# Longformer attention and its feed-forward stage on one core: transposes between another pair's score products, clears on ScalarE, one scatter per batch, casts spread by pair

## The chip, the core and the metric

The kernel runs on one core of a Trainium2 chip. The core has TensorE (PE, with its weight loads as PEld), VectorE (DVE), ScalarE (ACT), GpSimd (POOL) and SyncE (SP), each with a queue of its own that it takes in order; SP and POOL issue the DMAs. The metric is the time of one execution on the device in microseconds, lower is better; a kernel's time is the median of several runs.

## The reference

```python
# q, k, v: [8 batches, 8 heads, 576 positions, 64], global_idx: 8 positions
scores = matmul(q, k.T) / 8
mask = (abs(i - j) <= 32) | is_global[i] | is_global[j]
attn = softmax(where(mask, scores, -1e9))
x = matmul(attn, v)                  # to [4608 tokens, 512]
r = maximum(x @ w_in, 0)             # w_in [512, 2048]
out = (s * r * r + b) @ w_out        # w_out [2048, 512]
```

## The kernel before

**Tiling.** A *pair* is two heads of one batch; pairs are numbered 0 to 31, four to a batch. A pair's keys lie in five chunks of 120, with the 8 global rows put in front of each. For each chunk one score product (`qk`, L449) multiplies the chunk's keys `kt` with a window of the pair's queries `qbd`; ScalarE takes the exponential (`e`), VectorE multiplies with the mask (`em`). Then `pv` (L476) makes 28 products: `em` with V and with ones, into one PSUM tile `po`. `norm_steps` follow: logarithm of the sums on ScalarE (`ln`), its negative exponential (`rep`), and on VectorE the normalised output into `xt`, plus `gs`, the sums for the global queries.

**Preparation of a pair.** `trans_a` and `trans_b` transpose K and Q of a pair on PE into a PSUM tile `pst`; VectorE, and for batches 0 and 1 ScalarE for half of q, evacuate it to `kt` and `qbd`. For batches 0 and 1 `select_globals` and `select_v` pick the global rows by products (`psg`, `psv`), and a small DMA on SP puts the selected rows of V (`gv`) into `vx`. Three `qbd` buffers hold zeros in the half that belongs to the other head, and rows 0 to 7 of `natv` are zero at first; memsets on VectorE write these.

**Loads.** K and Q of batches 0 and 1 come through POOL's DMA queue, already cast (`load_six`). From batch 2 on, SP loads K, Q and V in float32 to `natk`, `natq`, `natv` (`fetch`: 40 loads of half a batch's heads each, and three fills with the global rows that 24 gathers on POOL have put aside). ScalarE casts K and Q (L262), POOL casts V (L258).

**Second stage.** `moe_quanta` yields 288 quanta. For each of nine tiles of 512 tokens, 16 quanta compute `psh` (L546, four products or more, then ReLU on ScalarE and a square on VectorE) and 16 compute a quarter of `pso` (L561), with an output store on SP after each fourth. From pair 8 on, every pair runs eight of them, one behind each of its steps. The global queries' outputs are put into `xt` by the scatter in `finish_batch`: 8 small copies on POOL (L524), and a quantum that reads `xt` waits for them.

**Order.** All five engines take the order in which the code emits. `run_pair` has eight steps: five score products, `trans_a` of the next pair, `trans_b` and the selections, `pv`. What VectorE does for a step is put into `later` and emitted one step behind. The sums of w_out's rows for the bias need all of w_out in float32: eight pieces `wst`, two per pair in pairs 6 to 9, issued by SP into two buffers and added by VectorE a pair later (L698, L700).

Of the kernel before, what the change touches and what calls it, by code (L numbers as in the profile page):

```python
# [9 lines left out]
FP32 = mybir.dt.float32  # L10
# [53 lines left out]
def kernel(  # L64
# [96 lines left out]

    new_casts(0)
# [56 lines left out]
    nc.vector.memset(nat["v"][0:NG], 0.0)  # L219
# [266 lines left out]
    def norm_steps(p):  # L486
# [6 lines left out]

        def s1():
            nc.scalar.activation(ln[:], po[:, LQ : 2 * LQ], AF.Ln)  # L495
            later.append(
                lambda: nc.vector.tensor_reduce(
                    out=gs[:, hp],
                    in_=po.rearrange("p (h c j) -> p h j c", h=2, c=NCH)[:, :, HB : HB + NG, :],
                    axis=AX.X, op=OP.add,  # L500
                )
            )
# [278 lines left out]
```

## Time and profile before

| | |
|---|---|
| median of 3 runs | 420.28 us (420.23 to 421.6) |
| the profiled execution | 419.66 us, of which the trace's span is 418.0 us |
| PE busy | 355.6 us, 85% of the span |
| DVE busy | 243.7 us, 58% |
| ACT busy | 216.1 us, 52% |
| POOL busy | 67.2 us, 16% |
| mean granted clock of PE | 0.958 of full speed |

The three runs and the profiled execution lie within 0.5% of each other. The shares are averages over the whole span. The stretches, the waits and single instructions are in the rows further down: times count from the start of the span, "idle before" is what an engine waited just before an instruction, and behind the arrow stands what ended that wait.

### The profile page before, as it was taken

How to read it: one execution, taken by the hardware profiler on the slowest of the kernel's cores; microseconds unless marked ns; L12 is line 12 of the kernel's file. 1: busy time of each engine (PE TensorE's matmuls, PEld its weight loads, DVE VectorE, ACT ScalarE, POOL GpSimd, SP SyncE). 2: the span in 40 equal slices, each digit the busy share in tenths (PEclk: the TensorE clock that was granted, in tenths of full speed). 3: DMA queues.
4: the chain of work that ended last, by engine and by line, in shares of the span. 5: the costliest groups of instructions: out<-in, count | busy, mean ns of one | idle time of the engine just before them, and what ended most of it. 6: DMA issues, size and time to landing. Idle time of an engine off the chain costs nothing.

```text
span 418.0 us, 8890 instructions
## 1 busy us (share of the span) xinstructions
PE 355.6 (85%) x3323; PEld 215.0 (51%) x3354; DVE 243.7 (58%) x595; ACT 216.1 (52%) x401; POOL 67.2 (16%) x150
## 2 busy tenths in 40 slices
PE   2596483979925889989998999999999999999994
PEld 2364242544513545765685578557755764554442
DVE  5946272658607785875676577667666774332421
ACT  1346251666412853795488558836953872530610
POOL 5830595100211001110111020002101001000000
PEclk9998596999975999999999999999999999999999
DMA  8999625975895137953781587069601001101001
GB/s 153 177 206 211 110 39 119 151 199 159 155 164 160 45 126 152 147 143 88 151 181 48 126 161 181 1 146 154 169 27 51 27 2 52 50 2 76 26 32 69
DMA packets 113775, 46.33 MB, mean 111 GB/s; under 512 B 99044, under 2 KB 106212, under 8 KB 113732
## 3 DMA queue, kind: packets, MB, share of 16 engines
q1 hardware_dynamic: 105412, 38.91, 41.0%
q0 software_dynamic: 8320, 6.86, 10.5%
q8 instruction: 26, 0.43, 0.4%
q14 instruction: 17, 0.14, 0.1%
HBM read 42.77 MB, written 9.73 MB: 126 GB/s over the span
## 4 chain that ended last, share of the span: by engine, by line
PE 44%; issue 14%; SPq 13%; DMA 10%; DVE 8%; ACT 6%; POOL 3%; POOLq 0%; ACTq 0%; DVEq 0%
PE pso L561 23%; PE psh L546 14%; SPq L295 7%; SPq L306 6%; DMA natk<-in_k_dram 4%; PE po L476 3%; ACT r L553 3%; PE pss L449 3%; DMA win_t<-in_moe_w_in_dram 3%; DMA natv<-in_v_dram 2%; DVE g L556 2%; DVE qbd L397 2%; PE pst L360 2%; ACT e L453 1%; DVE wsum L700 1%
## 5 line engine op out<-in xcount | busy, mean ns | idle before, releaser
L546 PE MATMUL psh<-xt,win_t 128*128 128x512 bf16 (+7 forms) x1018 | 147.1, 290 | 12.3 <-POOL xt L524 11.6
L561 PE MATMUL pso<-wout_t,g 128*128 128x512 bf16 x551 | 137.7, 379 | 2.6 <-issue 1.9
L553 ACT ACTIVATE r<-psh 128x512 bf16<-128x512 f32 x144 | 87.4, 620 | 75.6 <-PE psh L546 73.7
L453 ACT ACTIVATE e<-pss 128x384 bf16<-128x384 f32 (+1 forms) x160 | 75.4, 483 | 83.7 <-PE pss L449 68.7
L546 PEld LDWEIGHTS <-win_t 128*128 128x128 bf16 x1024 | 85.8, 99 | 61.0 <-issue 21.8
L556 DVE TENSOR_TENSOR g<-r 128x512 bf16<-128x512 bf16 x144 | 64.9, 455 | 53.8 <-ACT r L553 51.8
L561 PEld LDWEIGHTS <-g 128*128 128x128 bf16 x576 | 54.1, 98 | 59.4 <-issue 3.5
L456 DVE TENSOR_TENSOR em<-e,mask 128x384 bf16<-128x384 bf16 (+1 forms) x160 | 55.3, 348 | 28.7 <-ACT e L453 27.0
L449 PE MATMUL pss<-qbd,kt 128*128 128x384 bf16 (+1 forms) x160 | 51.2, 331 | 16.3 <-ACT e L453 8.7
L575 DVE SCALAR_TENSOR_TENSOR osb<-pso,s_bc,bias_row 128x512 f32<-128x512 f32 x32 | 23.9, 748 | 42.0 <-PE pso L561 42.0
L524 POOL COPY xt<-xg 128x4 bf16 x72 | 15.2, 210 | 181.5 <-DVE xg L522 177.5
L258 POOL CAST vx<-natv 128x1280 bf16<-128x1280 f32 (+1 forms) x20 | 21.3, 1077 | 98.5 <-DMA natv<-in_v_dram 45.7
L397 DVE COPY qbd<-pst 64x640 bf16<-64x640 bf16 (+1 forms) x56 | 29.4, 525 | 0.3
L507 DVE TENSOR_TENSOR xt<-po,rep 128x600 bf16<-128x600 f32 x32 | 25.0, 781 | 6.8 <-ACT rep L505 6.8
L449 PEld LDWEIGHTS <-kt 128*128 128x128 bf16 x160 | 15.7, 100 | 25.1 <-DVE qbd L397 6.3
L495 ACT ACTIVATE ln<-po 128x640 f32<-128x640 f32 x32 | 22.5, 705 | 5.4 <-PE po L476 5.4
L505 ACT ACTIVATE rep<-ln 128x640 f32<-128x640 f32 x32 | 24.4, 764 | 0.1
L476 PEld LDWEIGHTS <-vx 128*64 128x64 bf16 x448 | 17.0, 118 | 14.3 <-issue 5.1
L476 PE MATMUL po<-em,vx 128*64 128x160 bf16 (+3 forms) x448 | 21.7, 237 | 2.5 <-DVE xt L507 1.6
L476 PE MATMUL po<-em,onesb 128*64 128x160 bf16 (+2 forms) x448 | 21.4, 237 | 0.0
L360 PE MATMUL pst<-ident,cq 128*128 128x128 bf16 x120 | 10.8, 222 | 11.7 <-ACT e L453 11.7
L700 DVE TENSOR_TENSOR wsum<-wsum,wst 128x512 f32<-128x512 f32 x14 | 9.6, 685 | 14.4 <-DMA wst<-in_moe_w_out_dram 14.4
(77 smaller groups left out, 209.9 us busy)
## 6 DMA issues: line engine op xcount, KB each, us to landing
out_dram<-osb SPq DMA_DIRECT2D x32, 256.0 KB
natq<-in_q_dram SPq DMA_DIRECT2D x108, 60.0 KB
natk<-in_k_dram SPq DMA_DIRECT2D x48, 120.0 KB
natv<-in_v_dram SPq DMA_DIRECT2D x48, 120.0 KB
wst<-in_moe_w_out_dram SPq DMA_DIRECT2D x8, 512.0 KB
natv<-in_v_dram SPq DMA_DIRECT2D x16, 150.0 KB
win_t<-in_moe_w_in_dram POOLq DMA_DIRECT2D x4, 512.0 KB, 10.0
wout_t<-in_moe_w_out_dram POOLq DMA_DIRECT2D x4, 512.0 KB, 12.8
```

The costliest lines, as they stand in the source:

```text
L295: eng.dma_start(out=nat[t][NG : NG + n, c, h0 : h0 + nh], in_=src[t][bi, h0 : h0 + nh, KC * c : KC * c + n].rearrange("h s d -> s h d"),)
L306: eng.dma_start(out=nat["q"][r : r + n, c, h0 : h0 + nh], in_=q[bi, h0 : h0 + nh, a : a + n].rearrange("h s d -> s h d"),)
L397: eng(out=o, in_=i)
L449: nc.tensor.matmul(ps[:], ktile[p][:, P * c : P * c + P], qbufs[p % 3][:, :, LO[c] : HI[c]])
L453: nc.scalar.activation(e[:], ps[:], AF.Exp, scale=SCALE)
L456: later.append(lambda: nc.vector.tensor_mul(em[:], e[:], masks[c]))
L476: nc.tensor.matmul(po[D * hh : D * hh + D, a : a + n], onesb[:] if part else vx[:, c, 2 * hp + hh], emt[(p, c)][:, hh, x : x + n], start=k ...
L507: lambda: nc.vector.tensor_tensor(out=xt[:, hp].rearrange("p (c a j) -> p c a j", c=NCH, a=2), in0=halves(po[:, 0:LQ]), in1=halves(rep[:]) ...
L546: nc.tensor.matmul(psh[:, d0 : d0 + n], win_t[:, a, f * P : f * P + P], xts[bi][:, a, x0 : x0 + n], start=(a == 0 and j == 0), stop=(a == ...
L553: nc.scalar.activation(r[:], psh[:], AF.Relu)
L556: later.append(lambda g=g, r=r: nc.vector.tensor_mul(g[:], r[:], r[:]))
L561: nc.tensor.matmul(pso[:], gl[f][:, u * P : u * P + P], wout_t[:, f], start=(f == 0), stop=(f == 15),)
```

## The change

`first_pair` replaces `run_pair` for batch 0: the next pair's transposes and selections stand between this pair's score products, and for pairs 0 to 4 the transposes' PSUM tile comes from the pool of the second stage. ScalarE clears `qbd` and `natv` by copies of a zero column. Pair 4 is prepared right behind batch 0, with no quantum ahead of it; batch 0 is scattered once, before pair 4 (before: there and again in pair 4). The memset of `natv`'s last rows goes. Loads of V for batch 1 are spread over pairs 1 to 3. `wst` is issued on POOL's queue. `fetch` takes half a batch at a time, and the casts of K and Q, two heads at a time, move to the last pair of the batch before and the first of the same batch. In batch 1 six quanta run per pair (before: four ahead of pair 4, then five per pair).

```diff
+    zero = const.tile([P, 1], FP32)
+    nc.vector.memset(zero[:], 0.0)
+
+    def clear(ap, n):
+        nc.scalar.copy(out=ap, in_=view(zero[0 : ap.shape[0]], [0, n]))
+
+    def clear_q(t):
+        clear(t[0:D, 1], LQ)
+        clear(t[D:P, 0], LQ)
+
+    clear_q(qbufs[0])
+    clear(nat["v"][0:NG].rearrange("p c h d -> p (c h d)"), NCH * H * D)
+    clear_q(qbufs[1])
+    clear_q(qbufs[2])
...
-    nc.vector.memset(nat["v"][0:NG], 0.0)
...
-    nc.vector.memset(qbufs[0][0:D, 1], 0.0)
-    nc.vector.memset(qbufs[0][D:P, 0], 0.0)
...
-    cast_v(G, 0, 0, 2)
     for hp in (2, 3):
         load_six("k", 0, hp)
         load_six("q", 0, hp)
+    cast_v(G, 0, 0, 2)
     cast_v(G, 0, 2, 2)
-    for j in range(4):
+    for j in range(2):
         nc.gpsimd.dma_start(
-            out=win_t[:, :, 512 * j : 512 * j + 512],
-            in_=w_in2[:, :, 512 * j : 512 * j + 512],
+            out=win_t[:, :, 1024 * j : 1024 * j + 1024],
+            in_=w_in2[:, :, 1024 * j : 1024 * j + 1024],
         )
...
     def trans(t, p):
         bi, hp = divmod(p, 4)
-        ps = ps_s.tile([P, LQ], BF16, tag="s", name="pst")
+        if p < 5:
+            ps = ps_m.tile([P, LQ], BF16, tag="moe", name="pst")
+        else:
+            ps = ps_s.tile([P, LQ], BF16, tag="s", name="pst")
...
-    def finish_batch(bi):
-        xt, gs = xts[bi], gsums[bi]
-        xg = nrm.tile([P, 4, NG], BF16, tag="xg", name="xg", bufs=2)
-        rec = nrm.tile([P, 4, NG], FP32, tag="rec", name="rec", bufs=1)
-        nc.vector.reciprocal(out=rec[:], in_=gs[:, :, 1])
-        nc.vector.tensor_tensor(out=xg[:], in0=gs[:, :, 0], in1=rec[:], op=OP.mult)
+    def scatter(bi):
+
         for i in range(NG):
             nc.gpsimd.tensor_copy(
-                out=xt[:, :, ds(greg_p[i], 1)], in_=xg[:, :, i : i + 1]
+                out=xts[bi][:, :, ds(greg_p[i], 1)], in_=xgs[bi][:, :, i : i + 1]
             )
...
             elif s == 5:
-                if hp == 0 and bi > 0:
-                    later.append(lambda: finish_batch(bi - 1))
+                if hp == 0 and bi > 1:
+                    later.append(lambda: scatter(bi - 1))
...
+    def first_pair(p):
+
+        if p == 0:
+            open_batch(0)
+        for s in range(NCH):
+            prev, later[:] = list(later), []
+            qk(p, s)
+            if s in (0, 2):
+                step()
+            if p < 3:
+                if s == 1:
+                    trans_a(p + 1)
+                elif s == 2:
+                    trans_b(p + 1)
+                    select_globals(p + 1)
+                elif s == 3:
+                    select_v(p + 1)
+            for f in prev:
+                f()
+        flush()
+        pv(p)
+        pending.extend(norm_steps(p))
...
-    def casts_for(bi):
-
-        return (
-            {1: [lambda: cast(A, "k", bi, 0, HG)], 4: [lambda: cast(A, "q", bi, 0, HG)],
-             5: [lambda: cast_v(G, bi, 0, HG)]},
-            {1: [lambda: cast(A, "k", bi, HG, HG)], 4: [lambda: cast(A, "q", bi, HG, HG)],
-             5: [lambda: cast_v(G, bi, HG, HG)]},
-        )
+    def casts_for(bi, h0):
+
+        c = lambda t, h: (lambda: cast(A, t, bi, h, 2))
+        return {
+            0: [c("k", h0)], 2: [c("q", h0)], 5: [c("k", h0 + 2)], 6: [c("q", h0 + 2)],
+            4: [lambda: cast_v(G, bi, h0, HG)],
+        }
...
-    for t in qbufs[1:]:
-        nc.vector.memset(t[0:D, 1], 0.0)
-        nc.vector.memset(t[D:P, 0], 0.0)
     for p in range(4):
-        run_pair(p, Z, p < 3)
-        if p == 2:
-            for h in range(H):
-                load_v_head(1, h)
+        first_pair(p)
+        for h in ((), (0, 1), (2, 3, 4), (5, 6, 7))[p]:
+            load_v_head(1, h)
+    cast_v(G, 1, 0, 2)
+    step()
+    trans_a(4)
     flush()
-    while pending:
-        step()
-        flush()
-    finish_batch(0)
+    step()
+    trans_b(4)
+    flush()
+    select_globals(4)
+    select_v(4)
+    scatter(0)
+    flush()
...
-    for t in "kqv":
+    for t in "kq":
         nc.vector.memset(nat[t][PADROW:P, NCH - 1], 0.0)
...
     quanta[0] = 32
-    for _ in range(3):
-        Q()
-        flush()
-    trans_a(4)
-    trans_b(4)
-    select_globals(4)
-    select_v(4)
-    Q()
-    flush()
...
-        nc.sync.dma_start(out=wt[:], in_=w_out2[:, 2 * j : 2 * j + 2])
+        nc.gpsimd.dma_start(out=wt[:], in_=w_out2[:, 2 * j : 2 * j + 2])
...
         if bi == 1:
-            nq = [0, 1, 1, 0, 1, 0, 1, 1]
+            nq = [0, 1, 1, 1, 0, 1, 1, 1] if hp else [0, 0, 1, 1, 1, 1, 1, 1]
...
+        if hp == 3 and bi + 1 < B:
+            new_casts(bi + 1)
+            ex = casts_for(bi + 1, 0)
+        if hp == 0 and bi > 1:
+            ex = casts_for(bi, HG)
         if p == 5:
-            new_casts(2)
-            fetch(2)
-        if hp >= 2 and bi + 1 < B:
-            ex = casts_for(bi + 1)[hp - 2]
+            fetch(2, 0)
+        elif p == 6:
+            fetch(2, HG)
+        elif bi > 1 and hp < 2 and bi + 1 < B:
+            fetch(bi + 1, HG * hp)
         if p in (7, 8, 9, 10):
             more, adds = adds, []
-            for s, f in zip((2, 3, 6, 7), more):
+            for s, f in zip((1, 3, 4, 7), more):
                 ex.setdefault(s, []).append(f)
```

What moves is shown at three places of the order, for each before and then with the change. The numbers behind names are buffers.

VectorE in pair 1, from its first mask product to what it does for pair 2 (`kt`, `qbd` and the selected rows from `psg`; `gv`), before:

```order
L456 TENSOR_TENSOR em_496<-e,mask_344 128x320
L456 TENSOR_TENSOR em_501<-e,mask_346 128x384
L497 TENSOR_REDUCE gs<-po 128x16
L456 TENSOR_TENSOR em_508<-e,mask_348 128x384
L456 TENSOR_TENSOR em_515<-e,mask_350 128x384
L507 TENSOR_TENSOR xt<-po,rep 128x600
L456 TENSOR_TENSOR em_522<-e,mask_352 128x320
L375 COPY kt<-pst 128x5x120
L397 COPY qbd_111<-pst 64x5x2x60
L415 CAST kt<-psg 128x5x8
L420 CAST qbd_111<-psg 64x5x8 x2
L439 CAST gv<-psv 8x128
```
With the change:

```order
L470 TENSOR_TENSOR em_496<-e,mask_348 128x320
L509 TENSOR_REDUCE gs<-po 128x16
L470 TENSOR_TENSOR em_502<-e,mask_350 128x384
L389 COPY kt<-pst 128x5x120
L470 TENSOR_TENSOR em_525<-e,mask_352 128x384
L528 TENSOR_TENSOR xt<-po,rep 128x600
L411 COPY qbd_111<-pst 64x5x2x60
L429 CAST kt<-psg 128x5x8
L434 CAST qbd_111<-psg 64x5x8 x2
L470 TENSOR_TENSOR em_573<-e,mask_354 128x384
L453 CAST gv<-psv 8x128
L470 TENSOR_TENSOR em_592<-e,mask_356 128x320
```
The evacuations for the next pair stood behind the pair's last mask product; now they stand between the mask products, and the last one comes behind `gv`.

SP from the first half's fills in batch 2's fetch on, before (`vx` from `gv` is the small DMA for pairs 6 and 7, `wst` a piece of w_out):

```order
L326 DMA natk<-gsk 8x5x512
L326 DMA natq<-gsq 8x5x512
L326 DMA natv<-gsv 8x5x512
L295 DMA natk<-in_k_dram 120x4x64 x4
L295 DMA natk<-in_k_dram 96x4x64
L306 DMA natq<-in_q_dram 60x4x64 x9
L306 DMA natq<-in_q_dram 36x4x64
L295 DMA natv<-in_v_dram 120x4x64 x4
L295 DMA natv<-in_v_dram 96x4x64
L440 DMA vx_108<-gv 8x5x128
L696 DMA wst<-in_moe_w_out_dram 128x2x512 x2
L440 DMA vx_108<-gv 8x5x128
```
With the change, from the small DMAs for pairs 4 and 5 on:

```order
L454 DMA vx_108<-gv 8x5x128 x2
L306 DMA natk<-in_k_dram 120x4x64 x4
L306 DMA natk<-in_k_dram 96x4x64
L317 DMA natq<-in_q_dram 60x4x64 x9
L317 DMA natq<-in_q_dram 36x4x64
L306 DMA natv<-in_v_dram 120x4x64 x4
L306 DMA natv<-in_v_dram 96x4x64
L337 DMA natk<-gsk 8x5x256
L337 DMA natq<-gsq 8x5x256
L337 DMA natv<-gsv 8x5x256
L454 DMA vx_108<-gv 8x5x128
```
The small DMA for pair 6 stood behind both halves of the fetch and now stands behind the first; the pieces `wst` are no longer in SP's queue.

POOL behind the 24 gathers of batch 1, before: the end of the second scatter of batch 0 (`xt_358`), the casts of V for batch 2 and the start of batch 1's scatter (`xt_997`):

```order
L524 ISA
L524 COPY xt_358<-xg_1119 128x4
L258 CAST vx0_107<-natv_106 128x5x256 x2
L524 ISA
L524 COPY xt_997<-xg_1833 128x4
```
With the change, from the last gather on; `xt_960` is batch 1's output:

```order
L329 DMA gsv_276<-in_v_dram 6x8x64
L726 DMA wst_1383<-in_moe_w_out_dram 128x2x512
L726 DMA wst_1385<-in_moe_w_out_dram 128x2x512
L726 DMA wst_1571<-in_moe_w_out_dram 128x2x512
L726 DMA wst_1573<-in_moe_w_out_dram 128x2x512
L269 CAST vx0_107<-natv_106 128x5x256
L726 DMA wst_1714<-in_moe_w_out_dram 128x2x512
L726 DMA wst_1716<-in_moe_w_out_dram 128x2x512
L269 CAST vx0_107<-natv_106 128x5x256
L539 ISA
L539 COPY xt_960<-xg_1754 128x4
```
The second scatter is gone, and the pieces `wst` stand in this queue, two of them ahead of the cast and the scatter of batch 1.

## Rows read from the trace of the kernel before

**Rows 1.** Windows (from:to, length, busy us and instructions): seven stretches

```profile
core 0: us, PE busy (x) PEld busy (x) DVE busy (x) ACT busy (x) POOL busy (x), PEclk, DMA share, GB/s
0.00:12.87 12.87, 3.10 (x58) 2.61 (x58) 7.95 (x27) 1.94 (x2) 8.08 (x21) 1.00 0.95 158
12.87:22.62 9.75, 6.65 (x90) 4.49 (x90) 7.60 (x20) 2.78 (x6) 7.43 (x11) 1.00 1.18 182
22.62:42.88 20.26, 15.63 (x215) 10.07 (x214) 12.11 (x33) 10.85 (x23) 2.23 (x3) 0.89 1.24 208
42.88:57.20 14.32, 7.37 (x73) 3.62 (x74) 6.23 (x18) 4.49 (x7) 10.75 (x23) 0.68 0.53 82
57.20:110.62 53.42, 42.32 (x460) 23.73 (x468) 32.70 (x85) 27.56 (x52) 15.45 (x34) 0.94 0.66 142
110.62:143.63 33.01, 19.84 (x180) 11.80 (x179) 14.60 (x36) 15.33 (x29) 3.06 (x5) 0.79 0.62 140
143.63:155.82 12.19, 10.45 (x81) 5.29 (x82) 10.65 (x24) 7.58 (x13) 0.00 (x0) 1.00 0.23 87
```

**Rows 2.** Windows: two pairs without casts, two with casts

```profile
311.48:330.14 18.66, 18.34 (x178) 11.50 (x179) 12.04 (x31) 9.68 (x20) 1.62 (x8) 1.00 0.15 57
174.48:194.81 20.33, 19.21 (x187) 11.85 (x188) 14.42 (x35) 16.19 (x28) 1.25 (x1) 1.00 0.37 96
```

**Rows 3.** Timeline (start, us, engine, line, operation) of the start

```profile
6.49 2.19 DVE L219 MEMSET natv<- 8x2560 f32 x1 [0.46 <-issue]
...
8.08 0.69 PE L348 MATMUL pst<-ident,cq 96*64 96x96 bf16 x12 [1.03 <-DMA cq<-in_q_dram]
...
11.37 0.76 DVE L397 COPY qbd<-pst 64x600 bf16<-64x600 bf16 x1
...
12.16 0.65 ACT L397 COPY qbd<-pst 64x600 bf16<-64x600 bf16 x1 [10.00 <-DVE qbd L397]
...
12.80 2.58 DVE L246 SCALAR_TENSOR_TENSOR mask<-band,notg,gadd 128x160 bf16<-128x160 f32 x5
```

**Rows 4.** Windows: one pair of batch 0

```profile
23.58:31.16 7.58, 6.76 (x90) 4.55 (x90) 4.73 (x14) 3.83 (x9) 1.48 (x2) 1.00 1.27 206
```

**Rows 5.** Timeline between batches 0 and 1

```profile
41.43 0.53 PEld L476 LDWEIGHTS <-vx 128*64 128x64 bf16 x14 [2.76 <-DMA vx<-gv]
...
45.88 2.05 POOL L524 COPY xt<-xg 128x4 bf16 x8 [17.30 <-DVE xg L522]
...
53.48 0.48 DVE L680 MEMSET natv<- 32x512 f32 x1 [6.35 <-POOL vx L258]
...
57.50 1.03 PE L546 MATMUL psh<-xt,win_t 128*128 128x512 bf16 x4
...
66.71 2.06 POOL L524 COPY xt<-xg 128x4 bf16 x8
...
68.82 0.58 PE L546 MATMUL psh<-xt,win_t 128*128 128x512 bf16 x1 [6.17 <-POOL xt L524]
```

**Rows 6.** Timeline: SP's loads of batch 2 and pair 6

```profile
65.31 2.55 SPq L295 DMA_DIRECT2D natk<-in_k_dram  x5
...
89.56 0.72 SPq L440 DMA_DIRECT2D vx<-gv  x1
...
91.74 0.61 PE L476 MATMUL po<-em,vx 128*64 128x160 bf16 x14 [0.92 <-DMA vx<-gv]
```

**Rows 7.** Timeline: DVE and PE in pair 9

```profile
127.80 0.69 DVE L700 TENSOR_TENSOR wsum<-wsum,wst 128x512 f32<-128x512 f32 x1 [14.35 <-DMA wst<-in_moe_w_out_dram]
...
129.34 0.69 PE L360 MATMUL pst<-ident,cq 128*128 128x128 bf16 x5 [11.72 <-ACT e L453]
```

**Rows 8.** The tile of the weights w_out: issues and landing

```profile
L288 POOL DMA_DIRECT2D wout_t<-in_moe_w_out_dram x4: 742/744/764, 21.4 to 27.8; - x4
...
DMA to landing us min/median/max: 11.7/12.8/13.0
```

**Rows 9.** The chain that ended last (start, us, what): the wait for wst

```profile
124.12 3.59 DMA wst<-in_moe_w_out_dram
```

More of the change, by code (lines that the diff above doesn't have):

```diff
@@ L160, in load_v_head @@
         )
+    zero = const.tile([P, 1], FP32)
[9 more added lines that the diff above has]
+    clear_q(qbufs[2])
+    onesb = const.tile([P, D], BF16)
+    nc.vector.memset(onesb[:], 1.0)
     new_casts(0)
@@ L235 @@
     nc.vector.tensor_tensor(out=notg[:], in0=vkey[:], in1=isg[:], op=OP.is_gt)
-    nc.vector.memset(qbufs[0][0:D, 1], 0.0)
-    nc.vector.memset(qbufs[0][D:P, 0], 0.0)
-    onesb = const.tile([P, D], BF16)
-    nc.vector.memset(onesb[:], 1.0)
     masks = []
@@ L321, in gather, with fill @@
             )
-    def fill(t, bi):
+    def fill(t, bi, h0, nh):
         r = HB if t == "q" else 0
-        s = gsc[t][bi].rearrange("g h d -> g (h d)")
+        g = gsc[t][bi].rearrange("g h d -> g (h d)")[:, D * h0 : D * (h0 + nh)]
         nc.sync.dma_start(
-            out=nat[t][r : r + NG].rearrange("p c h d -> p c (h d)"),
-            in_=view(s, [0, NCH], [1, H * D]),
+            out=nat[t][r : r + NG, :, h0 : h0 + nh].rearrange("p c h d -> p c (h d)"),
+            in_=view(g, [0, NCH], [1, D * nh]),
         )
-    xts, gsums = {}, {}
+    xts, gsums, xgs = {}, {}, {}
     ktile, emt, otile = {}, {}, {}
@@ L492, in norm_steps, with sums @@
         rep = nrm.tile([P, LQ], FP32, tag="rep", name="rep")
+        def sums():
+            nc.vector.tensor_reduce(
+                out=gs[:, hp],
+                in_=po.rearrange("p (h c j) -> p h j c", h=2, c=NCH)[:, :, HB : HB + NG, :],
+                axis=AX.X, op=OP.add,
+            )
+            if hp == 3:
+                rec = nrm.tile([P, 4, NG], FP32, tag="rec", name="rec", bufs=1)
+                xg = nrm.tile([P, 4, NG], BF16, tag="xg", name="xg", bufs=2)
+                xgs[bi] = xg
+                nc.vector.reciprocal(out=rec[:], in_=gs[:, :, 1])
+                nc.vector.tensor_tensor(out=xg[:], in0=gs[:, :, 0], in1=rec[:], op=OP.mult)
         def s1():
             nc.scalar.activation(ln[:], po[:, LQ : 2 * LQ], AF.Ln)
[L496 to L500, printed above, removed]
-                )
-            )
+            later.append(sums)
         def s2():
@@ L598, in step, with open_batch, run_pair @@
             pending.pop(0)()
-    def run_pair(p, nq, trans_next, extra=None):
+    def open_batch(bi):
+        xts[bi] = xtp.tile([P, 4, 2 * HB * NCH], BF16, tag="xt", name="xt")
+        gsums[bi] = nrm.tile([P, 4, 2, NG], FP32, tag="gs", name="gs")
+    def run_pair(p, nq, trans_next, extra):
         bi, hp = divmod(p, 4)
         if hp == 0:
-            xts[bi] = xtp.tile([P, 4, 2 * HB * NCH], BF16, tag="xt", name="xt")
-            gsums[bi] = nrm.tile([P, 4, 2, NG], FP32, tag="gs", name="gs")
+            open_batch(bi)
         for s in range(8):
@@ L625, in run_pair @@
                 pending.extend(norm_steps(p))
-            for f in (extra or {}).get(s, ()):
+            for f in extra.get(s, ()):
                 f()
@@ L674 @@
         load_six("q", 1, hp)
-    for hp in range(4):
+    for hp in range(1, 4):
         cast_v(G, 1, 2 * hp, 2)
@@ L678 @@
     nc.vector.memset(onesf[:], 1.0)
-    for t in "kqv":
+    for t in "kq":
         nc.vector.memset(nat[t][PADROW:P, NCH - 1], 0.0)
@@ L744 @@
     Q(quanta[0])
-    finish_batch(B - 1)
+    scatter(B - 1)
     quanta[0] += 64
```

25 lines of the change are left out of this document (8 added, 17 removed).

## The prediction

> **What bounds the kernel now.** I read the cut into stretches first [rows 1], because TensorE (PE) is nearly full in the late part and the page's average hides where it is not: two late pairs of heads at 311 to 330 us keep it busy for 18.34 of 18.66 us [rows 2]. Before 143.6 us PE is busy for 94.91 of 143.63 us (the sum of the first six stretches of [rows 1]). So there the question is which wait ends last, place by place.
>
> *Start.* The first score product runs at 12.87 us. The q transposes begin at 8.08 us, when the load lands. VectorE (DVE) was in a 2.19 us memset of `natv` from 6.49 on, so everything behind it in its queue, up to the evacuation of q at 11.37, came late; ScalarE's half of q follows that and ends at 12.81 [rows 3].
>
> *Batch 0.* From 22.62 to 42.88 us DVE works 12.11 and PE 15.63 of 20.26 us [rows 1]; one pair takes 7.58 us, 4.73 of them DVE work [rows 4]. Neither is full: it is a chain of score, exp, mask, transposes, evacuation, value product. The last value product also waits 2.76 us for a small DMA [rows 5].
>
> *Between the batches.* The scatter runs from 45.88 to 47.93 on GpSimd (POOL), and PE waits for it. Then DVE's memset of `natv` starts only at 53.48, behind POOL's casts, and holds the evacuations of pair 4. Then the scatter of batch 0 runs a second time: behind 24 gathers it starts at 66.71, and PE idles for 6.17 us [rows 5].
>
> *Batches 1 and 2.* SyncE (SP) issues the 40 loads of batch 2 between the 65.31 and the 89.56 row, and only then the small DMA on which pair 6's value product waits until 91.74 [rows 6]. Later DVE waits 14.35 us for a piece of w_out (127.80), ScalarE waits for DVE, and PE stands for 11.72 us until 129.34 [rows 7].
>
> *Later batches.* The two pairs in which ScalarE casts K and Q take 20.33 us, two without casts 18.66 [rows 2].
>
> **The change part by part.** I work against the profiled execution: 418.0 us of span and 1.66 us around it make 419.66, which is 0.62 below the median of 420.28.
>
> *Start: 2.5 us less.* The memsets leave DVE, so q is evacuated as soon as its transposes end. These start at 8.08 and take about 0.85, DVE's half 0.76, ScalarE's half 0.65 [rows 3]: 10.4 instead of 12.87. ScalarE now does the clears: four of 640 and one of 2,560 columns. At 0.65 us for 600 columns [rows 3] that is some 5.5 us, and ScalarE is idle for 10.9 of its first 12.87 us [rows 1], with q's half due at 9.7. If that cover were short, each microsecond over would be one later.
>
> *Pair 0: 0.8 us less.* The 2.58 us of mask building stay [rows 3]; four memsets between the masks and the first product leave DVE. The next pair's transposes no longer stand behind all five score products: with their own PSUM pool they run between them, and their evacuations between the mask products. POOL's casts of V now fall beside the mask building, which takes some back. I take 8.9 us for 9.75 [rows 1], with bounds of 7.9 (casts free) and 9.75 (nothing gained).
>
> *Pairs 1 to 3: 0.4 us more.* The interleaving puts kt, qbd and the selected rows in DVE's queue ahead of the last mask product, for which the value product waits; before, they ran under the value product. So DVE's 4.73 us of a pair [rows 4] stay in series with the value product, the next score product and its exp, for which DVE idles 7.58 - 4.73 = 2.85 us now: 7.6 a pair. The last pair has no transposes to evacuate (two copies like the 0.76 of [rows 3] and small ones, about 2.1): 5.5. Its 2.76 us DMA wait [rows 5] goes, because that DMA is issued a pair ahead of its use. 7.6 + 7.6 + 5.5 = 20.7 for 20.26 [rows 1]. So I expect no gain from the part that the title names first. Bounds: 18.5 (the evacuations hide after all) and 23.
>
> *To pair 4's first score product: 9.7 us less.* Before, 14.32 us [rows 1]: logarithm, reciprocal, scatter, four quanta of the second stage, transposes, a late memset, evacuations. Now pair 4's transposes come right behind the value product, evacuations follow the normalisation, no quantum stands ahead, and the memset of `natv` is gone. From the end of the value product (42.88 [rows 1]) to the scatter's start (45.88 [rows 5]) logarithm, reciprocal, normalising and selected sums take 3.0 us; kt's evacuation fits into the waits in it. Behind it come q's two halves, 0.76 and 0.65 [rows 3], and some 0.2 of gaps: 4.6. The scatter lies beside this: its input no longer waits for the normalising, and its 2.05 us [rows 5] end before the first quantum.
>
> *Pairs 4 to 8: 3.4 us less.* Before 53.42 us with PE busy for 42.32 [rows 1]. The four moved quanta come in here. At 1.03 us for a quantum of four products [rows 5]: 42.3 + 4.1 = 46.4. To it come waits. SP no longer has all 40 loads ahead of pair 6's DMA, but half a batch (about 11.5 us by [rows 6], and three fills). The DMA of pair 7 still stands behind the second half; counted from pair 4 it lands about 2 us after the value product wants it, if SP meets no other wait. I take 2 for that and 1.6 for ScalarE and DVE: 50.0. The second scatter's 6.17 us and the memset's hold are in this difference. Bounds: 46.4 and 55.
>
> *Pairs 9 and 10 up to the value product: 12.7 us less.* Before 33.01 us at a granted clock of 0.79 [rows 1], so partly at the lower level of 1.2 GHz. The pieces of w_out go to POOL's queue, one pair ahead of their additions, with no loads in front, so DVE's 14.35 us wait [rows 7] goes. Two pairs [rows 2] less a value product and a quantum are 18.7 - 1.9 = 16.8. A new wait comes: the pieces' two buffers make POOL wait for the addition in the last step of pair 8, and behind that DMA (0.74 us [rows 8]) stand a cast of V (1.25 [rows 2]) and the scatter of batch 1 (2.05 [rows 5]), on which pair 9's first quantum waits. 4.05 less the 1.3 that PE has left to do is 2.7, and I add 0.8 for a fall of the clock (the lower level doubles a product's time): 20.3. Bounds: 16.8 and 24.
>
> *Pair 11: 0.9 us less. Later batches: 5.3 us less.* The casts move from the pairs with ReLU quanta to pairs without them, in halves. The excess is 20.33 - 18.66 = 1.67 us a batch [rows 2], in four later batches. I keep 1.3 of it, since the halves add four fixed costs a batch and three more fills on SP: 5.3. Bounds: 0 and 6.7. Pair 11 (12.19 us [rows 1]) had one such pair.
>
> The sum: 2.5 + 0.8 - 0.4 + 9.7 + 3.4 + 12.7 + 0.9 + 5.3 = 34.9 us. 419.66 - 34.9 = 384.8, and against the median 385.4. I say **385**.
>
> *A rule against the change.* The wait for a piece of w_out issued by SP shows 3.59 us in the chain [rows 9]; POOL's issues of the same weights landed 11.7 to 13.0 us later, beside many other loads [rows 8]. The Trainium skill, in "SBUF — State Buffer", section "SBUF: two separate sides", says that descriptors of a DMA from the GpSimd queue are written by GpSimd's cores, which are locked out while VectorE runs one of its two-port modes, and advises issuing from SP or ScalarE instead. By that rule the pieces would land later on their new queue; no run here shows it by itself. With a piece's lead of about 5 us my sum has no wait for it; if they took 13 us the rival below holds.
>
> **The rivals.**
>
> *Pieces of w_out land late.* If a piece lands 13 us after its issue [rows 8], DVE, which takes its work in order, stands for about 13 - 5.5 = 7.5 us in pairs 8, 9 and 10 each, as it did in [rows 7]: up to 22 us back, 407; for a landing of 9 us about 10 back, 395. For it: the queue and [rows 8]. Against: those landings had DMA shares of 1.18 to 1.24, and pairs 4 to 8 have 0.66 [rows 1].
>
> *Slower than before.* The same mechanism has to give back 34.9 us, that is 11.6 in each of the three pairs, so it decides from landings of about 17 us; at 20 it costs 43 and gives 428. The longest landing in [rows 8] is 13.0.
>
> *SP stays late.* If the loads wait for each other as between 65.31 and 89.56, the DMAs of pairs 6 and 7 come 3 to 5 us later each and the casts of batch 2 hold ScalarE: 393.
>
> *The interleaving costs more.* With 23 us in pairs 1 to 3 and nothing won in pair 0: 388.
>
> *More than forecast.* If neither the scatter of batch 1 nor pair 7's DMA is waited for, and the later batches reach 18.66: 385 - 2.7 - 0.8 - 2 - 1.4 = 378; with the best end of batch 0 (2.2 + 1.0 better) 375.
>
> *The change does not do what it says.* The second scatter would have to be waited for anyway, by the gathers ahead of it. Against: the quanta read the same tile, complete after the first scatter. Worth 6 us: 391.
>
> **How the numbers follow.** Forecast (378 to 391, with dearer interleaving and a useless second-scatter removal inside it) 0.72; w_out late but under 17 us 0.09; SP late 0.06; better than forecast 0.10; slower 0.02; no effect 0.01. The open ends (4 us in the first three terms, 8 in pairs 4 to 8, 7 in pairs 9 and 10, 6 later) don't fall on one side together; a range of 374 to 398 leaves out the worse half of the late w_out and little else. A measurement of this kernel tells about 0.5% (2 us) from no change. Faster by over that 0.96, within it 0.02, slower 0.02.
>
> **What would show it.** Right: the first score product at about 10.4 us; pairs 1 and 2 still about 7.6 us apart; pair 4's first score product near 44; no idle of PE before a scatter in batch 1; a wait of 2 to 4 us for the scatter at the start of pair 9, near 94; pairs with casts under 9.6 us. Wrong: DVE waiting for wst in pairs 8 to 10; value products of pairs 6 and 7 waiting for vx over 3 us; batch 0's rounds clearly below 7 or above 8 us.

## The result, and the profile after

The changed kernel takes 401.94 us (median of 4 runs, 398.97 to 405.43) against 420.25 us: a ratio of 0.9544, 95% interval 0.9474 to 0.9613. One of the four runs (405.43) lies 1.6% above the fastest, counts as slow and is not in the ratio; the other three reach from 398.97 to 402.28. The kernel is faster, by 18 us where 35 were predicted; 401.94 lies outside the range (374 to 398). The profiled execution has a span of 400.0 us, against 418.0.

The same stretches as [rows 1] in the trace of the changed kernel, cut at the same events (the pairs' first score products; the end of pair 3's value product; the value products of pairs 10 and 11). Columns as there.

```profile
0.00:9.87 9.87, 3.03 (x58) 2.50 (x59) 5.20 (x24) 8.50 (x9) 8.33 (x21) 1.00 0.88 151
9.87:27.86 17.99, 6.61 (x90) 4.31 (x90) 5.23 (x17) 2.89 (x6) 2.43 (x4) 1.00 0.99 170
27.86:50.76 22.90, 17.53 (x217) 10.96 (x217) 11.84 (x33) 11.35 (x23) 6.24 (x9) 1.00 0.91 136
50.76:55.46 4.70, 3.01 (x61) 2.48 (x58) 3.54 (x11) 2.10 (x3) 1.05 (x6) 1.00 0.91 186
55.46:112.39 56.93, 48.11 (x484) 25.56 (x484) 36.69 (x89) 30.33 (x60) 24.99 (x42) 0.94 0.82 170
112.39:132.91 20.52, 17.31 (x180) 10.64 (x179) 16.75 (x36) 13.65 (x28) 6.46 (x13) 1.00 0.65 154
132.91:144.53 11.62, 10.66 (x81) 5.36 (x80) 10.47 (x25) 7.05 (x13) 0.00 (x0) 1.00 0.25 92
144.53:400.00 255.47, 251.02 (x2195) 153.44 (x2194) 152.91 (x356) 149.16 (x290) 20.83 (x56) 1.00 0.37 94
```

| stretch | before | predicted | after | after less predicted |
|---|---|---|---|---|
| start | 12.87 | 10.4 | 9.87 | -0.5 |
| pair 0 | 9.75 | 8.9 | 17.99 | **+9.1** |
| pairs 1 to 3 | 20.26 | 20.7 | 22.90 | **+2.2** |
| to pair 4 | 14.32 | 4.6 | 4.70 | +0.1 |
| pairs 4 to 8 | 53.42 | 50.0 | 56.93 | **+6.9** |
| pairs 9, 10 | 33.01 | 20.3 | 20.52 | +0.2 |
| pair 11 | 12.19 | 11.3 | 11.62 | +0.3 |
| the rest | 262.2 | 256.9 | 255.47 | -1.4 |

Five terms hold to within 1.4 us; three miss by 18.2 together. TensorE's waits in the changed kernel (engine, line, what was waited for: us in total, times, longest) name one cause for the three, the small DMA from `gv` to `vx` (the second row is the first load of K, as before):

```profile
PE po L490 <- DMA vx<-gv: 22.9, 4, 11.4
PE pst L362 <- DMA ck<-in_k_dram: 5.7, 1, 5.7
PE psh L561 <- POOL xt L539: 2.8, 1, 2.8
```

The four places, in the timeline (start, us, what; idle before and what ended it): the value products of pairs 0, 3, 6 and 7, and the scatter wait of pair 9.

```profile
26.12 1.01 PE L490 MATMUL po<-em,vx 128*64 128x160 bf16 x14 [11.38 <-DMA vx<-gv]
49.15 1.01 PE L490 MATMUL po<-em,vx 128*64 128x160 bf16 x14 [3.96 <-DMA vx<-gv]
84.82 0.61 PE L490 MATMUL po<-em,vx 128*64 128x160 bf16 x14 [1.02 <-DMA vx<-gv]
99.46 1.01 PE L490 MATMUL po<-em,vx 128*64 128x160 bf16 x14 [6.54 <-DMA vx<-gv]
115.52 1.00 PE L561 MATMUL psh<-xt,win_t 128*128 128x448 bf16 x7 [2.80 <-POOL xt L539]
```

Before, pair 0's value product didn't wait for this DMA at all, pair 3's waited 2.76 us [rows 5] and pair 6's 0.92 [rows 6]. It carries 10 KB. The chain of waits shows that most of a wait lies behind the issue, not ahead of it:

```profile
12.04 14.04 DMA vx<-gv
...
40.96 8.14 DMA vx<-gv
```

Pair 0's small DMA was issued at 12.04 us, 0.9 us earlier than before, and landed 14 us later. What else was under way then is in the timelines of POOL (first three rows) and SP of the changed kernel:

```profile
9.34 1.51 POOL L285 DMA_DIRECT2D win_t<-in_moe_w_in_dram  x2
13.41 0.72 POOL L269 CAST vx<-natv 128x640 bf16<-128x640 f32 x1 [2.55 <-DMA natv<-in_v_dram]
25.59 0.72 POOL L269 CAST vx<-natv 128x640 bf16<-128x640 f32 x1 [11.46 <-DMA natv<-in_v_dram]
```
```profile
1.33 6.57 SPq L154 DMA_DIRECT2D natv<-in_v_dram  x8
...
12.04 22.32 SPq L454 DMA_DIRECT2D vx<-gv  x3
34.41 1.20 SPq L154 DMA_DIRECT2D natv<-in_v_dram  x2
40.96 0.71 SPq L454 DMA_DIRECT2D vx<-gv  x1
```

The two loads of `win_t` are issued at 9.34 us. The last load of V, issued by SP before 7.9 us, lands only when POOL's cast starts at 25.59, and the small DMA stands behind it in SP's queue. So the theory to test was: **SP's queue, in which the small DMA stands, is starved by POOL's large weight loads (pair 0) or is long with other loads (pairs 3, 6, 7).** The rival: the small DMA is late for a reason of its own (its input, the casts, its issue), or any small DMA is late while the DMA engines are this full.

### The profile page after: what moved, and what is told of

It is laid out like the page before. It is cut to its first block, busy times and chain, and to the rows that moved or that the text cites. A ratio compares the mean times of both kernels' runs of the same rounds, so it can differ in the third digit from the quotient of the medians.

```text
span 400.0 us, 8942 instructions
## 1 busy us (share of the span) xinstructions
PE 357.3 (89%) x3354; PEld 215.3 (54%) x3354; DVE 242.6 (61%) x586; ACT 225.0 (56%) x432; POOL 70.3 (18%) x148
## 4 chain that ended last, share of the span: by engine, by line
PE 62%; DMA 11%; DVE 10%; SPq 7%; ACT 5%; issue 4%; POOL 1%; POOLq 0%; ACTq 0%
PE pso L576 28%; PE psh L561 21%; PE po L490 6%; DMA vx<-gv 6%; PE pss L463 4%; DMA natk<-gsk 3%; PE pst L374 2%; DVE g L571 2%; SPq L317 2%; SPq L306 2%; DVE qbd L411 2%; SPq L154 2%; DVE xt L528 1%; DMA natq<-in_q_dram 1%; ACT r L568 1%
## 5 line engine op out<-in xcount | busy, mean ns | idle before, releaser
L561 PE MATMUL psh<-xt,win_t 128*128 128x512 bf16 (+7 forms) x1024 | 144.9, 287 | 2.8 <-POOL xt L539 2.8
L576 PE MATMUL pso<-wout_t,g 128*128 128x512 bf16 x576 | 142.1, 381 | 0.0
L568 ACT ACTIVATE r<-psh 128x512 bf16<-128x512 f32 x144 | 88.7, 616 | 67.2 <-PE psh L561 62.6
L467 ACT ACTIVATE e<-pss 128x384 bf16<-128x384 f32 (+1 forms) x160 | 76.7, 484 | 76.6 <-PE pss L463 75.5
L571 DVE TENSOR_TENSOR g<-r 128x512 bf16<-128x512 bf16 x144 | 68.3, 475 | 40.4 <-ACT r L568 38.6
L470 DVE TENSOR_TENSOR em<-e,mask 128x384 bf16<-128x384 bf16 (+1 forms) x160 | 57.8, 364 | 34.4 <-ACT e L467 33.3
L463 PE MATMUL pss<-qbd,kt 128*128 128x384 bf16 (+1 forms) x160 | 53.0, 341 | 3.8 <-DVE gv L453 1.4
L490 PE MATMUL po<-em,vx 128*64 128x160 bf16 (+3 forms) x448 | 22.5, 237 | 23.9 <-DMA vx<-gv 22.9
L539 POOL COPY xt<-xg 128x4 bf16 x64 | 14.1, 220 | 130.1 <-DVE xt L528 126.4
L463 PEld LDWEIGHTS <-kt 128*128 128x128 bf16 x160 | 15.7, 100 | 18.2 <-issue 3.5
L273 ACT CAST cq<-natq 128x640 bf16<-128x640 f32 x24 | 17.5, 731 | 0.0
L273 ACT CAST ck<-natk 128x640 bf16<-128x640 f32 x24 | 17.4, 725 | 0.0
```

The costliest lines, as they stand in the source:

```text
L273: eng(out=natural(t, bi)[:, :, a:b], in_=nat[t].rearrange("p c h d -> p c (h d)")[:, :, a:b],)
L463: nc.tensor.matmul(ps[:], ktile[p][:, P * c : P * c + P], qbufs[p % 3][:, :, LO[c] : HI[c]])
L467: nc.scalar.activation(e[:], ps[:], AF.Exp, scale=SCALE)
L470: later.append(lambda: nc.vector.tensor_mul(em[:], e[:], masks[c]))
L490: nc.tensor.matmul(po[D * hh : D * hh + D, a : a + n], onesb[:] if part else vx[:, c, 2 * hp + hh], emt[(p, c)][:, hh, x : x + n], start=k ...
L561: nc.tensor.matmul(psh[:, d0 : d0 + n], win_t[:, a, f * P : f * P + P], xts[bi][:, a, x0 : x0 + n], start=(a == 0 and j == 0), stop=(a == ...
```

## The experiments

All edits are to the changed kernel unless another is named. The three times of it in the ratio spread over 3.3 us; a difference of 3 us to it is at the edge of what a time can tell, and there the traces decide.

### Pair 0: when the weights are loaded, and in how large pieces

**Weights behind the casts.**

```diff
-    for j in range(2):  # win_t
-        nc.gpsimd.dma_start(...)
     cast_v(G, 0, 4, 2)
     cast_v(G, 0, 6, 2)
+    for j in range(2):  # win_t
+        nc.gpsimd.dma_start(...)
```

> The changed kernel (401.94 us), with the two loads of win_t behind the last two casts of V in POOL's queue instead of ahead of them. Theory A: pair 0's value product waits 11.38 us because its small DMA stands in SP's queue behind loads of V whose small packets take turns with the large packets of win_t; without win_t beside them the loads of V land near 15 us and the value product starts near 16.5 instead of 26.1: about 9.5 us less, 392.5 (390 to 395), while pair 3 keeps a wait of 2 to 4 us. Rival B: the small DMA waits for something else (its row of gv, the casts on POOL, its own issue): value product still near 26, 402.

Measured 394.56 us (393.73 to 395.68). The value product of pair 0, in its timeline:

```profile
16.16 1.01 PE L490 MATMUL po<-em,vx 128*64 128x160 bf16 x14 [1.21 <-DMA vx<-gv]
```

It starts at 16.16 instead of 26.12, as theory A said, and rival B falls: its input and the casts that it needs are as they were, and the DMA is issued only 0.8 us earlier (11.20 for 12.04). Pair 0 now takes 7.83 us (10.08 to 17.91). Of the 10 us, 7.4 reach the end: the waits of pairs 6 and 7, for one, grow from 7.56 to 9.09 us together.

**Four pieces and eight pieces** in the same place of the queue:

```diff
-    for j in range(2):
+    for j in range(4):   # and, in the other kernel, range(8)
         nc.gpsimd.dma_start(
-            out=win_t[:, :, 1024 * j : 1024 * j + 1024],
+            out=win_t[:, :, 512 * j : 512 * j + 512],   # and 256
```

> The changed kernel, with win_t loaded in four pieces as before the change, in the same place of POOL's queue: the same bytes in packets of half the size. Theory A, in the form that two queues take turns packet by packet: the loads of V land near 19 to 20 us instead of 25.5, pair 0's value product starts near 20, 396 (394 to 398). Rival C (the queues share by bytes or by order of issue, the size of a packet doesn't matter): value product at 25 to 27, 401 to 403.

> The changed kernel, with win_t loaded in eight pieces in the same place of POOL's queue, packets a quarter of the size. Turns packet by packet: the value product of pair 0 (26.12 with two pieces, 21.64 with four, 16.16 with the loads behind the casts) starts near 19 (18 to 20), 396 (394 to 398.5). Rival: the size below four pieces doesn't matter, value product at 21 to 22, 398 to 399.5.

Measured 398.53 us with four, 395.35 with eight. The value product of pair 0:

```profile
21.64 1.01 PE L490 MATMUL po<-em,vx 128*64 128x160 bf16 x14 [6.54 <-DMA vx<-gv]
```
```profile
19.70 1.01 PE L490 MATMUL po<-em,vx 128*64 128x160 bf16 x14 [4.85 <-DMA vx<-gv]
```

So the size of a piece does count, at the same bytes and the same place: 26.12, 21.64, 19.70 us. The DMA view of the window from 15 to 18 us tells why (queue: packets, MB, share of 16 engines; q0 is POOL's queue, q1 SP's); first two pieces, then four, then eight:

```profile
q0 software_dynamic: 276, 0.56, 99.0%
q1 hardware_dynamic: 265, 0.04, 15.7%
```
```profile
q0 software_dynamic: 472, 0.47, 91.9%
q1 hardware_dynamic: 440, 0.11, 28.0%
```
```profile
q0 software_dynamic: 818, 0.41, 98.5%
q1 hardware_dynamic: 726, 0.14, 43.1%
```

In each, the two queues move nearly the same number of packets: 276 and 265, 472 and 440, 818 and 726. Their sizes differ: 0.56 MB in 276 packets is 2.0 KB each on POOL's queue, then 1.0 and 0.5 KB, while SP's are 0.15 to 0.25 KB on average. So in these windows the queues take turns by the packet, and the larger POOL's packets are, the fewer bytes SP's queue moves in the same time: 0.04, 0.11, 0.14 MB. More pieces also keep POOL issuing longer (1.5, 3.0 and some 6 us), but that is not the reason: POOL's queue is full in the window in all three (99.0, 91.9, 98.5%). The Trainium skill, in "DMA: Bandwidth & Descriptors", section "Queues, rings and completion order", says that an engine takes its queues in turn and changes only after a whole packet; these three runs agree in the equal counts, though none shows that a packet of the profile is what the page calls one. Eight pieces came out as expected. Four pieces missed the stated 394 to 398 by 0.5 us (the value product came 1.6 later than expected); the order of the three is what the theory says and the rival (size doesn't matter) doesn't.

### The small DMA on a queue of its own

```diff
-            nc.sync.dma_start(
+            nc.scalar.dma_start(
                 out=vx[0:NG, :, 2 * hp : 2 * hp + 2]...
```

> The changed kernel, with the small DMA from gv to vx issued by ScalarE in place of SP, in pairs 0 to 7; nothing else moves. Theory A (what holds it is the queue behind other loads on SP): the waits of 11.38, 3.96, 1.02 and 6.54 us fall to 0 to 2 each; ScalarE itself will stand at pair 3's small DMA until the cast of the last heads of V near 26 us, so about 17 of 22.9 us come back: 385 (381 to 389). Rival B (the DMA engines are full and a small DMA waits on any queue): the four waits stay within 2 us of what they are, 400 to 403.

Measured 393.07 us (391.82 to 394.98). TensorE's waits and, in ScalarE's timeline, two issues and what stands behind them:

```profile
PE pss L463 <- ACT e L467: 10.8, 6, 6.1
...
PE po L490 <- DMA vx<-gv: 1.1, 1, 1.1
```
```profile
24.68 0.70 ACTq L454 DMA_DIRECT2D vx<-gv  x1
25.42 0.44 ACT L467 ACTIVATE e<-pss 128x320 bf16<-128x320 f32 x1 [9.31 <-POOL vx L269]
...
95.31 0.72 ACT L273 CAST ck<-natk 128x640 bf16<-128x640 f32 x1 [4.13 <-DMA natk<-in_k_dram]
```

The waits of TensorE for the small DMA fall from 22.9 to 1.1 us, in all four pairs: beside the same weights in the same pieces, a DMA on another queue lands in time. Theory A holds for the cause, and rival B (full engines hold any DMA) falls. But only 8.9 of the expected 17 us come back, while TensorE's waits for exponentials rise from 0.9 to 10.8 us. ScalarE takes its work in order, and now it is ScalarE that stands: 9.31 us at pair 1's small DMA (not at pair 3's, as expected), with the exponentials behind it (6.1 us of TensorE's time), and later 4.13 us for the loads of K for batch 2. The first wait ends in the moment in which the last load of V lands and lets POOL's last cast start, at 24.6 us.

**Both edits together.**

> The changed kernel with both edits: win_t's loads behind the last casts of V, and the small DMA from gv to vx issued by ScalarE. Theory A: ScalarE no longer stands at pair 3's small DMA (the last cast of V comes near 16 us instead of 25), so the value product of pair 3 starts near 36 instead of 43.6 (small DMA on ScalarE alone), and most of that stays: 387 (384 to 390). Rival F: the loads of batch 2 are bound by the DMA engines and don't come earlier, so ScalarE's wait for K in pair 8 (4.13 us with the small DMA on ScalarE alone) grows by what is won before: 391 to 394.

Measured 393.03 us: nothing beyond the small DMA's edit alone. That is rival F's number, but not its mechanism: ScalarE's wait for K didn't grow (3.72 us), because little was won ahead of it. Pair 3's value product starts at 42.98, not near 36. ScalarE again stood at a small DMA, for 7.48 us at pair 2's, and what ended that by the trace is a load of V. SP, which no longer waits for `gv`, had issued the V loads of batch 1 from 11.16 us on.

### SP's queue in pairs 4 to 8

**Fills behind all loads**, on top of the two edits:

```diff
         if p == 5:
-            fetch(2, 0)
-        elif p == 6:
-            fetch(2, HG)
+            fetch(2, 0, False)     # without the fills
+            fetch(2, HG, False)
+            for h0 in (0, HG):
+                for t in "kqv":
+                    fill(t, 2, h0, HG)
```

> As the two edits together, and in batch 2's fetch all 40 loads are issued first and the six fills behind them (before: the loads of the second half behind the first half's fills, which wait for the gathers on POOL). Theory A': SP stands at the fills until the last gather, near 73 us, with the second half's loads queued behind; with these loads about 10 us earlier ScalarE's wait for K in pair 8 goes: 4 us less than with the two edits alone, 383 (380 to 386). Rival F: the DMA engines bound these loads, and nothing changes (within 1.5 us).

Measured 388.08 us (387.35 to 390.8), 5 us less than with the two edits: the step is the size that theory A' gave, on a start that was 6 us too low. ScalarE's wait for K in pair 8 is gone, and pair 8's value product starts at 96.59 instead of 101.36. So the fetch was held by its fills, which wait for POOL's gathers, and not by the DMA engines: with the two edits SP issues the first half's fills at 62.56, 66.64 and 72.08 and the second half's first load at 72.39, with the fills last that load goes out at 60.88. This is a limit of the faster kernel; the changed kernel itself reaches its fills only at 76.94, when the gathers are done.

**V loads of batch 1 later**, on top of that:

```diff
-        for h in ((), (0, 1), (2, 3, 4), (5, 6, 7))[p]:
-            load_v_head(1, h)
+        if p == 3:
+            for h in range(H):
+                load_v_head(1, h)
```

> As with the fills last (388.08 us: win_t behind the casts of V, small DMA on ScalarE, fills behind all loads), and the eight loads of V for batch 1 written behind pair 3 instead of spread over pairs 1 to 3. The trace of the kernel with the fills last names a load of V as what ends a wait of 7.4 us that ScalarE has at the small DMA issued in pair 1, and TensorE stands for 4.9 us for it. Theory A'': with these loads behind, that wait goes: 4 to 5 us less, 383.5 (382 to 385.5). Rival I: the loads then land too late for pair 4's selections, and the wait moves there: 387 to 390.

Measured 388.25 us (387.82 to 389.49): no change, and ScalarE's wait is still there:

```profile
31.98 0.44 ACT L467 ACTIVATE e<-pss 128x320 bf16<-128x320 f32 x1 [7.50 <-DMA natv<-in_v_dram]
```

The theory falls in its remedy, and the rival's number came for another reason: pair 4's selections don't wait. SP still issues these loads from 11.46 us on: since the small DMA left its queue, nothing stands there between the V loads of batch 0 and these, so writing them later moved nothing. The order of instructions in the program shows where the wait is from (SP's row first, then ScalarE's; in brackets the semaphores that the DMA waits for):

```
L154 DMA natv_106<-in_v_dram 120x5x64 [waits DMAHW1_49]
L454 DMA vx0_107<-gv_580 8x5x128 [waits DMAHW1_49,DVE_49,Pool_49]
```

The program hands out eight semaphores in turn to the DMAs of SP and ScalarE together. ScalarE's small DMA gets one that a load of V on SP had before it, and has to wait until that load has landed. With the small DMA on ScalarE alone it is the same: pair 1's gets the semaphore of the last load of V for batch 0. A queue of its own was not fully its own. A kernel with separate semaphores was not tried.

**Four buffers for the pieces of w_out**, on top:

```diff
-    stage = ctx.enter_context(tc.tile_pool(name="stage", bufs=2))
+    stage = ctx.enter_context(tc.tile_pool(name="stage", bufs=4))
```

> As the previous kernel, with four buffers for the pieces of w_out instead of two. The prediction's theory of the 2.8 us for which TensorE waits for the scatter of batch 1: POOL stands at a piece until VectorE's addition frees a buffer, with a cast of V and the scatter behind it. With four buffers it doesn't stand: the wait goes, 2 to 3 us less than the previous kernel, 381 (379 to 383). Rival J: the scatter is late for another reason (its input from VectorE, the cast of V): within 1 us of the previous kernel.

Measured 387.69 us (386.89 to 388.82; ratio to the kernel before 0.9217, 0.9167 to 0.9267), the fastest of all, though not to be told from the two kernels above. The 2.65 us for which TensorE waited for the scatter are gone from its trace, as expected (the pair takes 9.45 us between value products instead of 13.85), so the buffer was the cause. They didn't reach the end: ScalarE's wait at pair 2's small DMA was 3.1 us longer in this execution (10.57), and pair 10 took 1.3 us more.

### The terms of the prediction, one by one

**The old order in batch 0** (`run_pair`, transposes behind all score products):

```diff
-        first_pair(p)
+        run_pair(p, [0] * 8, p < 3, {})
```

> The changed kernel, with batch 0 in the old order (all five score products of a pair, then the next pair's transposes and selections); all else as changed. The prediction's theory: interleaving gains 0.3 us in each of pairs 1 and 2 (7.29 against 7.58) and little in pair 0, where the wait for the small DMA ends last either way: 402 to 404. Rival D (interleaving is worth 2 us or more a pair and the waits have eaten it): 406 to 410.

Measured 404.9 us (403.69 to 405.89), 0.9 above the expected range. Pairs 1 and 2 take 7.50 and 7.76 us from first score product to first score product, against 7.29 with the interleaving, and pair 3's value product starts at 50.88 instead of 49.15. So the interleaving, the change's first named part, is worth some 0.2 to 0.5 us a pair and 1.7 up to pair 3, not the 2 a pair of rival D. In pair 3, 0.96 of the 1.7 is a longer wait for the small DMA (4.92 for 3.96).

**Clears on VectorE again.**

```diff
     def clear(ap, n):
-        nc.scalar.copy(out=ap, in_=view(zero[0 : ap.shape[0]], [0, n]))
+        nc.vector.memset(ap, 0.0)
```

> The changed kernel, with the clears of qbd and natv as memsets on VectorE again, at the same place of the program. The prediction's term for the start: without the clears on VectorE the first score product comes 2.5 us earlier; it should go back from 9.87 to about 12.5. Theory K: in the changed kernel this gain is eaten in pair 0, where the value product waits for a small DMA that lands near 26 us whatever the start: 401 to 403, no change. Rival: the start counts in full, 404 to 405.5.

Measured 404.76 us (402.36 to 405.28). The trace says theory K at the place itself, the time doesn't:

```profile
12.09 0.74 PE L463 MATMUL pss<-qbd,kt 128*128 128x320 bf16 x2 [0.67 <-DVE gv L453]
26.45 1.01 PE L490 MATMUL po<-em,vx 128*64 128x160 bf16 x14 [9.49 <-DMA vx<-gv]
```

The first score product is 2.2 us later than with the clears on ScalarE, pair 0's value product 0.33. But the waits of pairs 3 and 7 for the small DMA are 5.47 and 7.88 us here, 2.9 more than in the changed kernel; pair 0's is 1.9 shorter and pair 6's 1.0 is gone, so that all of them together stay at 22.8 for 22.9. Why the waits shift is not settled, and with a difference of 3 us neither is whether the gain at the start reaches the end.

**One scatter, alone, in the kernel before:**

```diff
-                if hp == 0 and bi > 0:
+                if hp == 0 and bi > 1:
                     later.append(lambda: finish_batch(bi - 1))
```

> The kernel before, without its second, repeated scatter of batch 0; all else as before. The prediction counted the 6.17 us for which TensorE waited for it as part of the gain in pairs 4 to 8: by that 414 (413 to 416). Rival G: SP's loads of batch 2, with the small DMA of pair 6 and the pieces of w_out behind them, don't come earlier; what is won at 66.71 is given back in pair 6 and at the latest in pair 9: 418.5 to 420.5.

Measured 421.41 us, a ratio of 1.0035 (1.0017 to 1.0053): 6.17 us of waiting [rows 5] taken away, nothing gained, a little lost. Pair 5's value product comes at 73.43 instead of 80.54 us, and in pair 6 all of it is given back, first in a score product that stands behind ScalarE's cast of K for batch 2 (this waits 3.56 us for K's fill, which SP loads), then at the small DMA:

```profile
83.17 0.43 PE L449 MATMUL pss<-qbd,kt 128*128 128x320 bf16 x1 [5.32 <-ACT e L453]
...
93.39 1.01 PE L476 MATMUL po<-em,vx 128*64 128x160 bf16 x14 [3.38 <-DMA vx<-gv]
```
The wait of VectorE for a piece of w_out in pair 9 stays too:

```profile
131.80 0.69 DVE L700 TENSOR_TENSOR wsum<-wsum,wst 128x512 f32<-128x512 f32 x1 [14.91 <-DMA wst<-in_moe_w_out_dram]
```

The small DMA of pair 6 and the pieces of w_out stand behind SP's 40 loads as before ([rows 6, 7]: 91.74 and 127.80), and these don't come earlier when TensorE is ready earlier. That is rival G, even beyond its 420.5.

**Pieces of w_out on SP again.**

```diff
-        nc.gpsimd.dma_start(out=wt[:], ...)
+        nc.sync.dma_start(out=wt[:], ...)
```

> The changed kernel, with the pieces of w_out issued by SP again, as before the change. The prediction's theory: the queue is what made VectorE wait (14.35 us before); behind half-batch loads on SP a piece lands some 5 to 10 us late in pairs 7 to 9, less the 2.80 us for the scatter, which then has no piece ahead of it on POOL: 407 (404 to 413). Rival H: the order of the loads in halves is enough, the queue of the pieces doesn't matter or costs: 399 to 402.

Measured 407.32 us (406.42 to 407.85). VectorE's waits for a piece return:

```profile
96.64 0.69 DVE L728 TENSOR_TENSOR wsum<-wst 128x512 f32<-128x512 f32 x1 [10.81 <-DMA wst<-in_moe_w_out_dram]
...
117.93 0.91 DVE L730 TENSOR_TENSOR wsum<-wsum,wst 128x512 f32<-128x512 f32 x1 [3.59 <-DMA wst<-in_moe_w_out_dram]
...
132.94 1.00 DVE L730 TENSOR_TENSOR wsum<-wsum,wst 128x512 f32<-128x512 f32 x1 [6.07 <-DMA wst<-in_moe_w_out_dram]
```

The queue it is; rival H falls.

## Why the prediction was right and wrong

**Right: the start.** 9.87 us for 10.4. The cover was thinner than said: the clears took 1.46 + 2.32 + 2.92 = 6.7 us of ScalarE, not 5.5, and it was idle for 0.37 us before q's half at 9.16.

**Wrong: pair 0 (17.99 for 8.9).** The step that failed is one that is missing. The sum priced VectorE's memsets and POOL's casts, but not the loads that the diff moves on POOL's queue: K and Q for pairs 2 and 3 ahead of the casts, and `win_t` in pieces of twice the size, issued at 9.34 instead of 12.62. The time was at nobody's instruction but in a queue: a 10 KB DMA with 14.04 us from issue to landing. No rival named it. With the weights behind the casts, and K and Q left where the change puts them, the stretch took 7.83 us, so the loads of `win_t` are the miss. Its work was priced 1.1 us too high: 7.83 is just under the lower bound of 7.9, with a wait of 1.21 us still in it.

**Wrong: pairs 1 to 3 (22.90 for 20.7), by one sentence.** "Its 2.76 us DMA wait goes, because that DMA is issued a pair ahead of its use." It was issued at 40.96, 4.2 us ahead of its need (before: at 36.8, 1.9 us ahead), but it landed 8.14 us later instead of 4.6, behind two loads of V that the change puts ahead of it on SP (34.41), while POOL's queue loaded the weights `wout_t`: a wait of 3.96. From 41 to 45 us the two queues move nearly equal numbers of packets, as in pair 0:

```profile
q0 software_dynamic: 637, 0.63, 93.6%
q1 hardware_dynamic: 589, 0.15, 27.9%
```
How much of the wait is the loads ahead and how much the weights beside them was not separated; on ScalarE's queue it was gone. The interleaving itself was priced on the safe side: 7.29 us a pair for 7.6, and 8.32 - 3.96 = 4.36 for pair 3 where 5.5 stood. Its gain is as small as the prediction said.

**Right: to pair 4's first score product.** 4.70 us for 4.6.

**Wrong in size: pairs 4 to 8 (56.93 for 50.0).** The mechanism stands in the prediction (pair 7's small DMA behind the second half of the fetch), with 2 us, whose working it doesn't show; it took 6.54, and pair 6 added 1.02. SP's second half took 79.38 to 94.24, 14.9 us for the 11.5 assumed ([rows 6] give 24.25 for both, 12.1 each), and the small DMA, issued at 94.34, another 5 to land. What made the half longer is in the chain that ended last:

```profile
76.94 6.79 DMA natk<-gsk
83.75 0.46 SPq L306
```
The fifth load of the half starts when K's fill from the first half lands. In the program that load takes the semaphore that the fill had, eight DMAs earlier, and so waits for it: five such loads took 4.83 us here. With the pieces of w_out back on SP's queue they took 2.54 and the half 12.4 us, so the pieces that the change puts on POOL's queue, beside this half, had a part in it. Without the two waits the stretch is 49.4, where 48 was said. The rival "SP stays late" had this with 3 to 5 us each, and a chance of 0.06; one of the prediction's own signs of being wrong, a wait of over 3 us for `vx` in pairs 6 and 7, was seen in pair 7.

The 6.17 us of the second scatter, counted as part of this term, were worth nothing when they alone were taken from the kernel before (421.41 us): whoever removes a wait ahead of a fixed arrival only waits there. The rival that called the removal useless gave a reason (the gathers) that is not the one seen.

**Right, in part by luck: pairs 9 and 10.** 20.52 us for 20.3, with the new wait named and sized: 2.80 us at the scatter for 2.7, and gone with four buffers. It came at 115.52, not near 94, since everything ahead was late. The clock fell to 0.94 in pairs 4 to 8 and stayed at 1.00 here, so the 0.8 us taken for it was not needed; without the new wait the stretch took 17.72 us where 16.8 was said, and by chance the 0.8 covers most of that.

**The rule against the change didn't act.** The pieces of w_out landed 3.9 to 7.1 us after POOL issued them (median 5.2), and VectorE never waited for one; issued by SP they cost 5 us more in all. The warning of the Trainium skill, "SBUF — State Buffer", section "SBUF: two separate sides", that VectorE's work can hold up DMAs from the GpSimd queue shows in no wait here.

**Right: pair 11 and the later batches.** 11.62 us for 11.3, and 6.7 us less for 5.3, of which 5.4 between the value products of pairs 12 and 31, where the casts were; the rest lies behind them.

## What to carry to other kernels

Price a moved load at the small transfers that share its queue or run beside it, not only at the instruction that waits for it: a transfer of 10 KB took 14 us behind loads of small packets that alternated with large ones. Before counting a removed wait as a gain, find the next arrival that doesn't depend on it; if that is fixed by a queue, the wait moves there. A small transfer that TensorE needs soon goes on a queue without bulk loads, issued by an engine that can afford to stand, and the semaphores it shares are part of its queue.

## What the runs showed of the hardware

- Two DMA queues that were both full moved nearly equal numbers of packets, though of different sizes: 276 and 265, 472 and 440, 818 and 726 in 3 us with POOL's packets at 2.0, 1.0 and 0.5 KB and SP's at 0.25 KB or less. Smaller pieces of the bulk load sped up the other queue: 26.12, 21.64, 19.70 us to the same point.
- The same 10 KB DMA on ScalarE's queue instead of SP's, with the same weights loaded beside it, cut TensorE's waits for it from 22.9 to 1.1 us; in exchange its waits for ScalarE's exponentials rose by 9.9 us. An issue took ScalarE 0.70 us, the first one 1.3.
